# Halving the last query chunk and opening each new key chunk with half of its heads, in a two-layer attention kernel

## The chip, the cores and the metric

The kernel runs on one core of a Trainium2 chip. The metric is the time of one execution on the device, in microseconds. All comparisons are of runs in the fast state. A ratio is the mean time of one kernel's fast runs over that of the kernel before in the same rounds, so it is not quite the ratio of the medians quoted beside it.

## The reference

The computation is four residual blocks over x of 2048 tokens by 1024 features: a linear-attention block A, softmax attention B, A again with the same weights, B again. Each starts with a layer norm without parameters. Both have 32 heads of 32 dimensions.

```python
def _A_ref(x, wqkv, w_phi, wo):            # linear attention
    q, k, v = qkv[0], qkv[1], qkv[2]       # of x @ wqkv
    pq = jnp.einsum("bhsd,hdf->bhsf", q, w_phi)
    pk = jnp.einsum("bhsd,hdf->bhsf", k, w_phi)
    phi_q = concat([softmax(pq), softmax(-pq)])
    phi_k = concat([softmax(pk), softmax(-pk)])
    kv = jnp.einsum("bhsf,bhsd->bhfd", phi_k, v)
    ...                                    # num / (den + 1e-6)
    return o @ wo

def _B_ref(x, wqkv, wo):                   # softmax attention
    scores = jnp.einsum("bhqd,bhkd->bhqk", q, k) * (Dh ** -0.5)
    p = softmax(scores)
    o = jnp.einsum("bhqk,bhkd->bhqd", p, v)
    return o @ wo

x = x + _A_ref(_layernorm(x), ...); x = x + _B_ref(_layernorm(x), ...)   # twice
```

## The kernel before

Tokens are handled in four chunks of 512. A prologue computes A's keys for all four. Then each of two "layers" interleaves the query side of A, the projections of B, B's attention and the key side of the next A. VectorE, ScalarE, TensorE and GpSimd run in the order in which the program emits; the order of the DMA queue is left to a scheduler.

Attention is a generator. Every `yield` ends one *step*: eight score matmuls, two exponentials of 128x1024, and, two steps later, sixteen matmuls for numerator and denominator (`ND`). A group `g` is four heads; there are eight.

```python
def block(self, q, k0, k1, acc, oT, first, last, before=None):
    kv = self.load(k0, k1, 0, acc, first)          # K and V of group 0 from DRAM
    for g in range(G):
        if before and g in before:
            before[g]()                            # finish what group g needs
            kv = self.load(k0, k1, g, acc, first)
        nxt = None
        for half in range(2):                      # 256 queries
            for kc in range(0, k1 - k0, 2):
                self.step(...)
                if nxt is None and g + 1 < G and not (before and g + 1 in before):
                    nxt = self.load(k0, k1, g + 1, acc, first)
                yield
        kv = nxt
```

All the rest is also generators, which yield how many matmuls of 512 columns they emitted and whether a PSUM buffer ended. `Background` gives them a credit per step, and `until` forces one to its end while no attention runs.

```python
def pump(self, per):
    self.credit = min(self.credit + per, 8.0)
    ends = 0
    while self.credit > 0 and ends < PS["nb"]:
        got = self.next()
        ...
        self.credit -= got[0]
        ends += got[1]

def attend(att, block, bg, per):
    for _ in block:
        bg.pump(per)
        if len(att.lag) > 1:
            att.finish()
```

K and V go to DRAM (`kT_d`, `v_d`), 512 KB for 16 heads of a chunk, and attention loads them group by group. PSUM has three layouts, with S score tiles and NB buffers for everything else: wide (0, 8), mid (2, 3), narrow (3, 1). The schedule of a layer, cut to what matters:

```python
bg.add("b0", b_proj(0, (1,)))
bg.add("b1", rest1())                                            # chunk 1: K, V and queries, all heads
attend(att, att.block(qs[0], 0, 4, ..., {4: lambda: bg.until("b0")}), bg, 10)
settle(att)
bg.until("b1")
set_mode("narrow")
bg.add("b2", to_b(2))                                            # query side of A, norm, K and V of chunk 2
bg.add("b3", to_b(3))
attend(att, att.block(qs[0], 4, 8, acc[0], None, False, False), bg, 5)
attend(att, att.block(qs[1], 0, 8, acc[1], None, True, False), bg, 5)
bg.until("b2")
attend(att, att.block(qs[0], 8, 12, ...), bg, 6)
attend(att, att.block(qs[1], 8, 12, ...), bg, 6)
bg.until("b3")
for i in range(NCH):
    ...                                                          # add next query chunk and after(i - 1)
    block = (att.block(qs[i], 0, S // P, None, oT[i], True, True) if i > 1
             else att.block(qs[i], 12, 16, acc[i], oT[i], False, True))
    attend(att, block, bg, 3.5)
settle(att)
bg.until(f"after{NCH - 2}")
set_mode("wide")
drain(after(NCH - 1, oT[-1], layer, True))                       # exposed: nothing left to hide it under
```

`after` is the follow-up of a chunk: output projection, then in the first layer the norm and A's key side, in the second the transposed store. In the prologue the norm of the next chunk is merged into the key side of the current one: one end of the norm per four ends of the key side.

The softmax here doesn't subtract the row's maximum and nothing guards it: scores larger than these inputs give would overflow.

Of the kernel before, what the change touches and what calls it, by code (L numbers as in the profile page):

```python
# [19 lines left out]
P = 128  # L20
# [4 lines left out]
G = 8  # L25
# [7 lines left out]
def kernel(  # L33
# [140 lines left out]
    def mm8(ps, lhsT, rhs):  # L174
        for po in range(G):
            mm(ps, lhsT(po), rhs(po), po == 0, po == G - 1)
            if po == 3:
                yield 4, False
# [3 lines left out]
    def ln_gen(x, res, fast=False):  # L182
        ps = ps512()
        yield from mm8(ps, lambda po: ones_bf[:], lambda po: x[:, po, :])
        m = T("f", [P, C], F32)
        DVE.tensor_scalar(out=m[:], in0=ps, scalar1=1.0 / D, scalar2=None, op0=ALU.mult)
        yield 4, True
        xc = T("c8", [P, G, C], BF16)
        res["xc"] = xc
        sqs = []  # L190

        def centre(po):
            DVE.tensor_tensor(out=xc[:, po, :], in0=x[:, po, :], in1=m[:], op=ALU.subtract)  # L193

        ps = ps512()
        for po in range(G):
            centre(po)
            if po % 4 == 0:
                sq4 = T("st", [P, 4, C], BF16)
            sq = sq4[:, po % 4, :]  # L200
            if fast:
                SC.activation(out=sq, in_=xc[:, po, :], func=ACT.Square)
            else:
                DVE.tensor_tensor(  # L204
                    out=sq, in0=xc[:, po, :], in1=xc[:, po, :], op=ALU.mult
                )
            sqs.append(sq)
        yield from wait(3)
        for po in range(G):
            mm(ps, ones_bf[:], sqs[po], po == 0, po == G - 1)  # L210
            if po < G - 1 and po % 2:
                yield 2, False
        lnv = T("f", [P, C], F32)
        rstd = T("r", [P, C], F32)
        SC.activation(out=lnv[:], in_=ps, func=ACT.Ln, scale=1.0 / D, bias=eps_t[:])
        SC.activation(out=rstd[:], in_=lnv[:], func=ACT.Exp, scale=-0.5)
        yield 2, True

        diag = T("f", [P, 4, P], F32)
        rcol = T("rcol", [P, 4], F32)  # L220
        DVE.tensor_tensor(
            out=diag[:], in0=rstd[:].rearrange("p (t q) -> p t q", q=P),
            in1=ident[:].unsqueeze(1).to_broadcast([P, 4, P]), op=ALU.mult,
        )
        DVE.reduce_sum(out=rcol[:], in_=diag[:], axis=AX.X)
        if fast:
            ncol = T("nc", [P, 4], F32)
            DVE.tensor_scalar(
                out=ncol[:], in0=rcol[:], scalar1=-1.0, scalar2=None, op0=ALU.mult
            )  # L230
            res["ncol"] = ncol
        res["rstd"], res["rcol"] = rstd, rcol
        yield from wait(1)
# [15 lines left out]
    def ak_gen(c, x, get, fast=False, res=None, hook=None):  # L249
        if c == 0:  # L250
            kv_state["acc"] = [T(f"acc{i}", [P, 4, 258], F32) for i in range(2)]
# [5 lines left out]
        SP.dma_start(out=xa_d[c][:], in_=xc[:])  # L257
        SP.dma_start(out=ra_d[c][:], in_=rstd[:])
        va = []
        for i in range(2):  # L260
            v = T(f"acc{2 + 2 * (c % 2) + i}", [P, 2, G, P + 1], BF16)
            POOL.memset(v[:, :, :, P:P + 1], 1.0)
            va.append(v)
        for fc in range(2):
            w = get()
            for t in range(4):
                ps = ps512()
                yield from mm8(
                    ps, lambda po: xc[:, po, t * P:(t + 1) * P], lambda po: w[:, po, :]
                )  # L270
                scale_rows(
                    va[t // 2][:, t % 2, fc * 4:(fc + 1) * 4, 0:P],
                    ps.rearrange("p (g d) -> p g d", d=P), rcol[:, t:t + 1], fast,
                )
                yield 4, True
# [3 lines left out]
        for fc in range(2):  # L279
            w = get()  # L280
            es = []
            for t in range(4):
# [33 lines left out]
            def kv_part(fc=fc, es=es):  # L316
                for gi in range(4):
                    g = fc * 4 + gi
                    ps = ps512()
                    for t in range(4):  # L320
                        for s in range(2):
                            mm(
                                ps[:, s * 129:(s + 1) * 129],
                                es[t][:, s, gi * P:(gi + 1) * P],
                                va[t // 2][:, t % 2, g, :],
                                t == 0 and s == 0, t == 3,
                            )
                    if c == 0:
                        DVE.tensor_copy(out=kvacc[fc][:, gi, :], in_=ps[:, 0:258])
                    else:  # L330
                        DVE.tensor_tensor(
                            out=kvacc[fc][:, gi, :], in0=ps[:, 0:258], in1=kvacc[fc][:, gi, :],
                            op=ALU.add,
                        )
                    yield 2.5, True
# [114 lines left out]
    def aq_gen(c, x, slabs, res, pause=6):  # L450
        xr = aq_load(c)
        slabs.prefetch()
        es = [T("ea", [P, 2, C], BF16) for _ in range(G)]
        yield from aq_exp(xr, slabs.get, es)
        yield from aq_scale(es, res)
        yield from wait(pause)
        yield from aq_out(es, res)
        yield from aq_finish(c, x, slabs, res)

    def aq_finish(c, x, slabs, res):  # L460
        yield from proj_out(x, res["oT"], slabs)
        yield from ln_gen(x, res, PS["ns"] == 0)
        SP.dma_start(out=x_d[c][:], in_=x[:])

    def proj_out(x, oT, slabs):
        for ft in range(G):
            if ft % 4 == 0:
                w = slabs.get()
            ps = ps512()
# [4 lines left out]
            yield 4, True  # L474


    def bkv_gen(c, res, slabs, h, q=None):
# [24 lines left out]
        if q is not None:  # L502
            yield from bq_gen(q, xc, rstd, slabs, range(4 * h, 4 * h + 4))
# [13 lines left out]
    class Attention:  # L517
# [22 lines left out]
        def block(self, q, k0, k1, acc, oT, first, last, before=None):  # L540

            kv = self.load(k0, k1, 0, acc, first)
            for g in range(G):
# [4 lines left out]
                for half in range(2):  # L548
# [161 lines left out]
    def run():  # L710
# [19 lines left out]
        drain(ln_gen(xs[0], res, True))  # L730
        for c in range(NCH):
# [12 lines left out]
            main = ak_gen(c, xs[c], iter(av + pk).__next__, True, res, hook)  # L744
            if c + 1 < NCH:
                xs[c + 1] = load_first(c + 1)
                drain(merge(main, ln_gen(xs[c + 1], nres, True), 4))
# [5 lines left out]
        def after(c, oT, layer, fast=False):  # L753
            x = load_x(c)
            sl = Slabs(["bo"] + (["av", "pk"] if layer == 0 else []))
            sl.prefetch()
            yield from proj_out(x, oT, sl)
            if layer == 0:
                yield from ak_gen(c, x, sl.get, fast)
                SP.dma_start(out=x_d[c][:], in_=x[:])  # L760
            else:
                yield from store_out(c, x)
# [8 lines left out]
        for layer in range(2):  # L771
# [4 lines left out]
            BKVQ = ["bk0", "bv0", "bq0", "bk1", "bv1", "bq1"]  # L776

            def to_b(c):
# [4 lines left out]
                yield from b_proj(c, (0, 1))  # L783
                SP.dma_start(out=xb_d[c][:], in_=res["xc"][:])
                SP.dma_start(out=rb_d[c][:], in_=res["rstd"][:])

            def b_proj(c, parts):
                res = saved[c]
                for h in parts:
                    yield from bkv_gen(c, res, res["sl"], h, qs.get(c))  # L790
# [5 lines left out]
            r0["sl"] = Slabs(["ao"] + BKVQ)  # L796
            r1["sl"] = Slabs(["ao"] + BKVQ)
# [19 lines left out]
            drain(b_proj(0, (0,)))  # L817

            def rest1():
# [3 lines left out]
                yield from b_proj(1, (0, 1))  # L823

            bg = Background()
            set_mode("mid")
            bg.add("b0", b_proj(0, (1,)))
            bg.add("b1", rest1())
            acc = [([T(f"acc{k}", [P, 2, 2, QH], F32) for k in range(4)], 0), None]
            attend(  # L830
                att,
                att.block(qs[0], 0, 4, acc[0], None, True, False, {4: lambda: bg.until("b0")}),
                bg, 10,
            )
            settle(att)
            bg.until("b1")
            acc[1] = ([T(f"acc{4 + k}", [P, 2, 2, QH], F32) for k in range(4)], 1)
            set_mode("narrow")
            bg.add("b2", to_b(2))
            bg.add("b3", to_b(3))  # L840
            attend(att, att.block(qs[0], 4, 8, acc[0], None, False, False), bg, 5)
            attend(att, att.block(qs[1], 0, 8, acc[1], None, True, False), bg, 5)
            bg.until("b2")
            attend(att, att.block(qs[0], 8, 12, acc[0], None, False, False), bg, 6)
            attend(att, att.block(qs[1], 8, 12, acc[1], None, False, False), bg, 6)
            bg.until("b3")
            oT = [None] * NCH
            for i in range(NCH):
# [3 lines left out]
                if i:  # L852
# [3 lines left out]
                block = (  # L856
                    att.block(qs[i], 0, S // P, None, oT[i], True, True) if i > 1
                    else att.block(qs[i], 12, 16, acc[i], oT[i], False, True)
                )
                attend(att, block, bg, 3.5)  # L860
            settle(att)
            bg.until(f"after{NCH - 2}")
            set_mode("wide")
            drain(after(NCH - 1, oT[-1], layer, True))
# [99 lines left out]
    def store_out(c, x):  # L964
        for t in range(4):
# [6 lines left out]
            SP.dma_start(out=out[0, c * C + t * P:c * C + (t + 1) * P, :], in_=tr[:])  # L972
# [35 lines left out]
```

## Time and profile before

| | |
|---|---|
| median time | 2828.98 us (2825.19 to 2832.77, 2 runs) |
| profiled span | 2830.9 us |
| PE busy | 84% |
| ACT busy | 76% |
| DVE busy | 47% |

The prediction below reads the main lines. Three stretches that it doesn't show are needed later: query chunk 0 on key chunks 1, 2 and 3 in the first layer. The columns are the stretch, its length, busy time and count of PE, weight load, DVE, ACT and POOL, then the granted PE clock, the DMA share and GB/s.

```profile
412.00:489.40 77.40, 59.33 (x1112) 27.87 (x1114) 34.35 (x61) 67.59 (x80) 0.00 (x0) 0.89 0.31 95
624.00:702.00 78.00, 55.57 (x1006) 24.67 (x995) 37.71 (x67) 63.56 (x73) 0.00 (x0) 0.85 0.22 67
805.00:870.00 65.00, 46.59 (x772) 20.33 (x776) 45.03 (x62) 58.58 (x64) 0.17 (x1) 0.84 0.37 107
```

In each of them ACT is busy 81% to 90% of the time and PE 71% to 77%. The DMA engines are busy for 22% to 37% of it, so they are far from full.

In the prologue, the timeline of PE shows that the matmuls which sum the squares for the norms of chunks 2 and 3 run without a wait ahead of them:

```profile
102.86 1.89 PE L165 MATMUL BG<-st,ones 128*128 128x512 bf16 x8
137.59 1.89 PE L165 MATMUL BG<-st,ones 128*128 128x512 bf16 x8
```

### The profile page before, as it was taken

What the parts mean: (1) busy time and instruction counts of PE and PEld (TensorE: products, weight loads), DVE (VectorE), ACT (ScalarE), POOL (GpSimd) and SP (SyncE); (2) the same over time, 40 slices, a digit from 0 to 9 for tenths busy, and PEclk for the clock granted to TensorE, in tenths of its full rate; (3) what the DMA queues carried; (4) which work ended last, traced back from release to release, by engine and by line L of the source; (5) the groups of instructions that cost most, each with busy time, mean ns of one, the idle gap of its engine ahead of it and who ended that gap; (6) DMA issues with size and microseconds to landing.
All of it is one profiled execution on the core that took longest, in us unless ns stands there. A gap on an engine that the chain in (4) does not pass through costs nothing. (4 is left out here: it accounts for less than half of the span.)

```text
span 2830.9 us, 89391 instructions
## 1 busy us (share of the span) xinstructions
PE 2375.8 (84%) x40048; PEld 1151.2 (41%) x40048; DVE 1326.5 (47%) x2205; ACT 2156.5 (76%) x2489; POOL 95.7 (3%) x87
## 2 busy tenths in 40 slices
PE   7988997996778879888778899799777778988877
PEld 4543443442333444444334344344333334434333
DVE  5776544425457653454524745444443773323213
ACT  5543728997668889898894354699874889999996
POOL 1320000000000010010101000000000000000000
PEclk9999998998998999999999999999888899999999
DMA  8424363342443422323105154425234242221110
GB/s 241 127 88 137 122 192 98 136 136 64 151 130 89 150 96 84 125 77 125 62 17 175 45 187 140 140 70 188 85 103 159 83 125 91 92 76 47 52 41 16
DMA packets 231392, 308.48 MB, mean 109 GB/s; under 512 B 36640, under 2 KB 194336, under 8 KB 223840
## 3 DMA queue, kind: packets, MB, share of 16 engines
q1 hardware_dynamic: 230192, 301.20, 33.5%
q8 instruction: 313, 5.13, 0.7%
q10 hardware_dynamic: 816, 1.57, 0.2%
q14 instruction: 71, 0.58, 0.1%
HBM read 239.14 MB, written 58.33 MB: 105 GB/s over the span
## 5 line engine op out<-in xcount | busy, mean ns | idle before, releaser
L576 ACT ACTIVATE E<-S 128x1024 bf16<-128x1024 f32 x2048 | 1911.8, 1149 | 369.4 <-PE S L567 368.5
L594 PE MATMUL ND<-E,kv 128*32 128x256 bf16 x8192 | 652.5, 286 | 246.5 <-DVE dt L614 98.8
L567 PE MATMUL S<-q,kv 32*128 32x256 bf16 x8192 | 570.2, 283 | 79.5 <-ACT E L576 43.0
L594 PE MATMUL ND<-E,ones 128*32 128x256 bf16 x8192 | 589.6, 286 | 0.0
L169 PE MATMUL BG<-c,w 128*32 128x512 bf16 x7680 | 482.1, 385 | 33.4 <-DVE x L473 14.7
L594 PEld LDWEIGHTS <-kv 128*32 128x32 bf16 x8192 | 278.7, 99 | 496.0 <-issue 311.5
L567 PEld LDWEIGHTS <-kv 32*128 32x128 bf16 x8192 | 177.3, 93 | 406.1 <-issue 403.5
L594 PEld LDWEIGHTS <-ones 128*32 128x32 bf16 x8192 | 271.7, 100 | 54.1 <-issue 5.2
L169 PEld LDWEIGHTS <-w 128*32 128x32 bf16 x7680 | 191.4, 97 | 240.1 <-issue 107.2
L632 DVE RECIPROCAL rc<-nd 128x256 f32<-128x256 f32 x128 | 224.4, 1753 | 4.4
L169 PE MATMUL BG<-w,c 128*32 128x512 bf16 x3328 | 212.9, 388 | 12.1 <-DVE st L239 5.1
L473 DVE TENSOR_TENSOR x<-BG,x 128x512 bf16<-128x512 f32 x128 | 87.1, 689 | 193.7 <-PE BG L169 175.4
L625 DVE COPY nd<-ND 128x512 f32<-128x512 f32 x64 | 44.1, 689 | 260.9 <-PE ND L594 260.6
L165 PE MATMUL BG<-c,w 128*128 128x512 bf16 x640 | 150.6, 396 | 1.6 <-DVE nd L625 1.6
L169 PEld LDWEIGHTS <-c 128*32 128x32 bf16 x3328 | 83.8, 97 | 105.3 <-issue 46.8
L306 POOL TENSOR_TENSOR ea<-ea,sm 128x512 bf16<-128x512 bf16 x64 | 93.4, 1459 | 776.8 <-ACT E L576 328.1
L165 PEld LDWEIGHTS <-c 128*128 128x128 bf16 x704 | 69.3, 99 | 86.3 <-issue 6.6
L165 PE MATMUL BG<-w,c 128*128 128x512 bf16 x448 | 99.4, 383 | 2.0 <-ACT st L924 2.0
L300 DVE TENSOR_REDUCE sm<-ea 128x32 f32<-128x1024 bf16 x64 | 77.8, 1215 | 48.2 <-ACT ea L296 35.0
L165 PEld LDWEIGHTS <-w 128*128 128x128 bf16 x640 | 64.5, 101 | 85.3 <-issue 17.5
L387 DVE TENSOR_TENSOR f<-BG,r 128x512 f32<-128x512 f32 x64 | 43.3, 689 | 106.6 <-PE BG L169 76.7
L486 DVE TENSOR_TENSOR st<-BG,r 128x512 bf16<-128x512 f32 x64 | 44.2, 691 | 97.7 <-PE BG L169 93.3
(110 smaller groups left out, 1584.6 us busy)
## 6 DMA issues: line engine op xcount, KB each, us to landing
w<-in_B_wqkv_dram SPq DMA_DIRECT2D x48, 1024.0 KB
dn<-den_d SPq DMA_DIRECT2D x320, 64.0 KB
x_d<-x SPq DMA_DIRECT2D x16, 1024.0 KB
x<-x_d SPq DMA_DIRECT2D x16, 1024.0 KB
w<-in_A_wo_dram SPq DMA_DIRECT2D x16, 1024.0 KB
w<-in_B_wo_dram SPq DMA_DIRECT2D x16, 1024.0 KB
kv<-kT_d SPq DMA_DIRECT2D x32, 512.0 KB
kv<-v_d SPq DMA_DIRECT2D x32, 512.0 KB
```

The source lines that it names most:

```text
L165: PE.matmul(ps, lhsT=lhsT, rhs=rhs, start=start, stop=stop, skip_group_check=True)
L169: PE.matmul(ps[cols, :], lhsT=lhsT[:, cols], rhs=rhs, start=start, stop=stop, tile_position=(0, 32 * j), skip_group_check=True,)
L300: DVE.reduce_sum(out=ss[:], in_=e[:].rearrange("p s (h f) -> p s h f", f=DH), axis=AX.X)
L306: (POOL if s else DVE).tensor_tensor(out=e[:, s, :].rearrange("p (h f) -> p h f", f=DH), in0=e[:, s, :].rearrange("p (h f) -> p h f", f=DH ...
L387: DVE.tensor_tensor(out=pq[:], in0=ps, in1=rstd[:], op=ALU.mult)
L473: DVE.tensor_tensor(out=x[:, ft, :], in0=ps, in1=x[:, ft, :], op=ALU.add)
L486: DVE.tensor_tensor(out=st[:, gi, :], in0=ps, in1=rstd[:], op=ALU.mult)
L567: PE.matmul(tiles[j // 2][:, o:o + QH], lhsT=kv[rows, 0, (kc + k) * P:(kc + k + 1) * P], rhs=q[rows, g, half * QH:(half + 1) * QH], start= ...
L576: SC.activation(out=e[:], in_=tiles[i][:].rearrange("p (j k q) -> p j k q", k=2, q=QH), func=ACT.Exp, scale=SCALE,)
L594: PE.matmul(nd[rows, part * QH:(part + 1) * QH], lhsT=ones_bf[:, 0:32] if part else kv[:, 1, col:col + 32], rhs=es[j // 2][:, j % 2, i, :] ...
L625: DVE.tensor_copy(out=ndc[:], in_=nd[:])
L632: DVE.reciprocal(out=rc[:], in_=ndc[:, QH:C])
```

## The change

It has two parts and some retuned numbers. **Part 1**: the last query chunk is attended in two halves of 256 queries, so that the follow-up of its first half runs beside attention of the second; everything in that follow-up takes a width `n` and an offset `o`. **Part 2**: of each new key chunk only K and V of the first 16 heads are made before its attention starts; those of the other heads come in the background and are needed at group 4. The queries of query chunk 1 (64 units, in the prediction's sense of a unit: four tile matmuls over 512 columns) go to the background with them, as `q1`. The numbers: the norm yields five empty turns rather than three, `pause` goes from 6 to 8, the credit of two blocks from 6 to 5 and of the last chunk's blocks from 3.5 to 4.

```diff
     def ln_gen(x, res, fast=False):
+        n = x.shape[2]                      # widths C become n throughout
...
-        yield from wait(3)
+        yield from wait(5)
...
-    def aq_gen(c, x, slabs, res, pause=6):
+    def aq_gen(c, x, slabs, res, pause=8):
...
-        def block(self, q, k0, k1, acc, oT, first, last, before=None):
+        def block(self, q, k0, k1, acc, oT, first, last, before=None, halves=(0, 1)):
...
-            bg.add("b1", rest1())
+            bg.add("b1a", rest1())          # rest1 now ends with b_proj(1, 0)
...
-            bg.until("b1")
+            bg.until("b1a")
...
-            bg.add("b2", to_b(2))
-            bg.add("b3", to_b(3))
-            attend(att, att.block(qs[0], 4, 8, acc[0], None, False, False), bg, 5)
+            bg.add("b1b", b_proj(1, 1))
+            bg.add("q1", b_query(1))
+            bg.add("b2a", to_b(2))
+            bg.add("b2b", rest_b(2))
+            bg.add("b3a", to_b(3))
+            bg.add("b3b", rest_b(3))
+            attend(att, att.block(qs[0], 4, 8, acc[0], None, False, False, need("b1b")), bg, 5)
+            bg.until("q1")
             attend(att, att.block(qs[1], 0, 8, acc[1], None, True, False), bg, 5)
-            bg.until("b2")
-            attend(att, att.block(qs[0], 8, 12, acc[0], None, False, False), bg, 6)
-            attend(att, att.block(qs[1], 8, 12, acc[1], None, False, False), bg, 6)
-            bg.until("b3")
+            bg.until("b2a")
+            attend(att, att.block(qs[0], 8, 12, acc[0], None, False, False, need("b2b")), bg, 5)
+            attend(att, att.block(qs[1], 8, 12, acc[1], None, False, False), bg, 5)
+            bg.until("b3a")
...                                         # key chunk 3: need("b3b") for query chunk 0
+                    for half in range(2):   # i == 3
+                        if half:
+                            bg.add("after3", chain(wait(3), after(3, oT[3], layer, n=QH)))
+                        block = att.block(
+                            qs[i], 0, S // P, None, oT[i], True, True, halves=(half,)
+                        )
+                        attend(att, block, bg, 4)
             settle(att)
-            bg.until(f"after{NCH - 2}")
+            bg.until("after3")
             set_mode("wide")
-            drain(after(NCH - 1, oT[-1], layer, True))
+            drain(after(NCH - 1, oT[-1], layer, True, QH, QH))
```

## The prediction

> **What bounds the kernel now.** I read the page first (busy table, groups), then busy time by stretch, then the PE and DMA-queue timelines at the seams between stretches.
>
> ```profile
> PE 2375.8 (84%) x40048; PEld 1151.2 (41%) x40048; DVE 1326.5 (47%) x2205; ACT 2156.5 (76%) x2489; POOL 95.7 (3%) x87
> ...
> L576 ACT ACTIVATE E<-S 128x1024 bf16<-128x1024 f32 x2048 | 1911.8, 1149 | 369.4 <-PE S L567 368.5
> ```
>
> No engine is full over the whole span; the stretches differ. One attention "step" is two exponentials (L576), eight score matmuls (L567) and sixteen ND matmuls (L594); 512 steps make a layer. Between steps the kernel slips in background matmuls (BG).
>
> ```profile
> 489.40:624.00 134.60, 126.14 (x2611) 64.99 (x2612) 50.09 (x92) 124.33 (x139) 0.00 (x0) 1.00 0.43 140
> 702.00:787.00 85.00, 68.08 (x1397) 34.24 (x1398) 35.63 (x71) 61.81 (x66) 0.00 (x0) 0.92 0.46 145
> 787.00:805.00 18.00, 13.07 (x228) 6.28 (x224) 4.63 (x7) 0.00 (x0) 0.00 (x0) 1.00 0.47 147
> 1404.00:1495.50 91.50, 71.58 (x1192) 31.95 (x1185) 17.22 (x18) 91.49 (x100) 0.00 (x0) 1.00 0.08 25
> 1496.90:1563.30 66.40, 58.34 (x304) 27.96 (x304) 36.63 (x57) 21.79 (x34) 11.69 (x8) 0.89 0.54 186
> 2804.00:2831.00 27.00, 20.84 (x106) 9.64 (x97) 12.73 (x43) 0.00 (x0) 0.00 (x0) 0.82 0.10 39
> ```
>
> The columns are stretch, length, busy PE, weight load, DVE, ACT, POOL, then PE clock, DMA share and GB/s. 1404 to 1495 is attention alone: ACT is full, two exponentials take 1.83 us, and PE has room. 489 to 624 has both: PE 94%, ACT 92%. 787 to 805, 1497 to 1563 and 2804 to 2831 hold no attention at all; nor does 367 to 412, below. These are what the change attacks.
>
> ```profile
> 371.29 5.35 PE L169 MATMUL BG<-c,w 128*32 128x512 bf16 x96
> 376.47 7.07 PE L169 MATMUL BG<-w,c 128*32 128x512 bf16 x128
> 383.38 13.98 PE L169 MATMUL BG<-c,w 128*32 128x512 bf16 x256
> 397.19 7.07 PE L169 MATMUL BG<-w,c 128*32 128x512 bf16 x128
> 404.10 7.07 PE L169 MATMUL BG<-c,w 128*32 128x512 bf16 x128
> ...
> 791.75 1.91 PE L169 MATMUL BG<-c,w 128*32 128x512 bf16 x32 [0.79 <-DVE st L486]
> 794.45 1.91 PE L169 MATMUL BG<-w,c 128*32 128x512 bf16 x32 [0.79 <-DVE st L486]
> ```
>
> I call four tile matmuls over 512 columns a unit; a product of eight is eight units. Chunk 1's forced work, with three PSUM buffers, flows at 7.07 us for 32 units, **0.221 us a unit**. Chunk 3's, with one buffer, repeats every 2.70 us for eight units, **0.34 us a unit**, since PE waits 0.79 us for each copy-out. Within attention, consecutive starts of L567 in the PE timeline give 0.88 us for a step with no unit that nothing delays, 1.74 to 1.84 us with four and 2.71 us with eight: 0.88 + 0.22 a unit, but never under ACT's 1.83. So four units a step are free, and a unit above that costs as much as an exposed one.
>
> **What the Trainium skill says.** TensorE: Matmul & The Clock Gate, "Wait — 56ns, not 53.3ns?", has warm matmuls of 512 columns 215.7 ns apart; the trace's 0.221 agrees. PSUM — Partial Sum Buffer, "Engine vs sequencer instructions", has matmuls in program order and VectorE's queue as strict FIFO. The trace agrees: a scale chain queued on DVE stops PE for 8.2 us behind an unrelated accumulator.
>
> ```profile
> PE ND L594 <- DVE dt L614: 8.2, 1, 8.2
> ```
>
> DMA: Bandwidth & Descriptors, "Anatomy of one DMA — SWDGE (gpsimd) path", says that the fixed cost is mostly the receipt of the write, and worst into HBM. That path is not this queue's, but the trace shows a long round trip too: V's write to DRAM is issued at 276.21 and its read back at 283.69.
>
> ```profile
> 276.21 0.53 SPq L501 DMA_DIRECT2D v_d<-st  x1
> 283.69 1.51 SPq L526 DMA_DIRECT2D kv<-v_d  x2
> ```
>
> **The change part by part.** I counted units around each block of steps in the built order of PE, identical in both layers unless said. First those forced with no attention, in units: before chunk 1's keys (4 to 8) 192 becomes 64; before chunk 2's keys 4 becomes 52; before chunk 3's keys 60 becomes 124; between the layers 584 becomes 468; at the very end 72 becomes 36.
>
> *Part 1, the last query chunk in halves.* The follow-up of the first half runs under the second half's 64 steps, which had 44 units in layer 1 and 0 in layer 2, and get 160 and 36, always under four a step.
> - Between layers, 66.4 us are exposed (1496.9 to 1563.3: projection 15.3, norm 8.6, V 15.2, phi(K) and kv the rest). With 256 queries: projection 64 x 0.11 + 0.8 = 8, norm about 5, V 32 x 0.218 = 7, kv 2, four softmax tiles of 2.3 us on DVE with their start 12, end 3: 37 us. That saves 29. The six weight slabs are loaded twice, though, and some 9 MB must land in 37 us, 243 GB/s against the 186 here, so I take 26.
> - Hidden work isn't free. The whole follow-up of chunk 2 held 78 steps for 174.5 us, against 78 x 1.83 = 143: 31.5 over. Half, less something for the longer norm wait, is 13. Net for layer 1: -13.
> - Tail: 27.0 us. The projection halves from 16.5 to 8, transposes and stores go from 9.5 to 5.5: -13. Hiding 36 units costs about 1. Net: -12.
> - K/V loads for the chunk double (8 MB more a layer) where DMA is 8% busy: nothing.
>
> Sum of part 1: **-25 us**.
>
> *Part 2, K/V of 16 heads first, for each layer.*
> - Before chunk 1's keys: 45.0 us from score to score become 0.88 + 64 x 0.221 = 15: -30.
> - Before chunk 2's: 52 x 0.34 = +17.
> - Before chunk 3's: 20.4 becomes 40 x 0.34 for the projection, 68 x 0.34 for K/V, and between them a norm whose 16 DVE operations and two PE passes nobody covers, about 14: 51. +30.
> - In the five blocks the counts are 86, 261, 58, 153, 0 before and 156, 168, 132, 56, 60 after, for 32, 64, 32, 32, 32 steps. Stepping through the new order with the durations of like steps of before (1.83; 2.10 mean at five units; 2.44 with a query-feature exponential; 10 for each scale chain), the blocks go from 77, 134, 77, 83, 65 to 75, 133, 83, 64, 70 us: -12. The 128 moved units push chunks 2 and 3 back by 26 steps, and what no longer fits reappears, slower, in the two later gaps.
>
> Sum: -30 + 17 + 30 - 12 = +5 a layer, **+10**. The longer waits (five for three in the norm, eight for six) spare perhaps 4 a layer of stalls such as the 2.9 us for squares in chunk 1: **-8**.
>
> **The rivals.**
> - *A DRAM round trip takes the place of the wait removed.* Before, the query projection (32 units, 7 us) or other heads' K/V stood between V's write and its first use. Now V is the last thing made before the first step of chunks 1, 2 and 3, and again at group 4 of chunk 3. 7.5 us from write to read and up to 3 for the read, less 3.5 of steps that PE can do, is 7 us each time, 28 a layer, 56 in all. For it: strict order on PE, and the build waits on that landing. Against: part of the 7.5 us was a 1 MB weight load issued just before. I take a third, **+18**. In full, the kernel lands near 2862.
> - *ACT is the bound throughout, and hidden work is free.* Then part 1 gains its 26 + 13 = 39 without the 14 of cost, and the blocks of part 2 shed some 15 more a layer, which turns +5 into -10: about -59, near 2770. Against: steps with five units already take 2.10 us, above 1.83.
> - *Weight traffic at the layer's end becomes the bound*, and the halved follow-up saves 15 rather than 26: +10 on my figure. DMA share was 0.54 there.
>
> **Range and chances.** -25 + 10 - 8 + 18 = -5: 2829 - 5 = **2824 us**. The round trip alone spans 0 to 56, the ACT rival reaches 2770; 2775 to 2870 should hold eight times in ten. 2% is 57 us, so faster needs nearly everything well: 0.14. Slower by 57 needs the full round trip and a failed part 1: 0.10. Within 2%: 0.76.
>
> **What would show it.** Right: no attention for about 15 us before chunk 1's keys, 17 before chunk 2's, 50 before chunk 3's; 40 rather than 66 us between last exponential and next layer's features; a tail near 14. Right for the rival: PE idle before the first ND of those blocks, ended by the V load. Wrong: gap three under 35 us, or second-half steps of the last chunk well above 1.95 us. A slot order on the DMA queue that holds K/V back would make me wrong towards slow; denominators landing earlier, hence fewer DVE stalls, towards fast.

## The result

The changed kernel takes 2912.19 us (2910.93 to 2913.46, 2 runs) against 2828.98 us: ratio 1.0294, interval 1.0232 to 1.0356. It is slower by 2.9%, outside the range that the prediction gave. The span of the profiled run is 2909.0 us against 2830.9, 78 us more. The interval is wide, some 18 us to either side, because each kernel ran only twice here. I found where the time went by the first and last exponential of each block of attention in the two traces (query chunk 0 on key chunk 0 in the first layer takes 87 us in both and is left out):

| stretch | before, us | after, us | difference |
|---|---|---|---|
| start to first attention step | 282.6 | 300.5 | +17.9 |
| layer 1: forced before key chunk 1 | 42.9 | 17.1 | -25.8 |
| layer 1: query chunk 0 on key chunk 1 | 76.9 | 90.7 | +13.8 |
| layer 1: query chunk 1 on key chunks 0 and 1 | 134.4 | 138.7 | +4.3 |
| layer 1: forced before key chunk 2 | 0.8 | 16.4 | +15.6 |
| layer 1: query chunk 0 on key chunk 2 | 77.2 | 90.8 | +13.6 |
| layer 1: query chunk 1 on key chunk 2 | 84.8 | 64.3 | -20.5 |
| layer 1: forced before key chunk 3 | 18.5 | 50.2 | +31.7 |
| layer 1: query chunk 0 on key chunk 3 | 65.4 | 84.1 | +18.7 |
| layer 1: rest of attention | 625.3 | 634.4 | +9.1 |
| between the layers | 162.7 | 135.4 | -27.3 |
| layer 2: first attention step to the end of query chunk 0 | 595.7 | 629.9 | +34.2 |
| layer 2: rest of attention | 549.8 | 550.4 | +0.6 |
| after the last step | 27.5 | 18.7 | -8.8 |

So part 1 gave what was promised (-27.3, -8.8, +9.1, +0.6). The prologue lost 18 us, and the stretch of part 2, from the first attention step to the end of query chunk 0, lost 52 us in the first layer (587.9 to 640.0) and 34 in the second.

The stretches of the changed kernel that answer to those of before, in the same columns: query chunk 0 on key chunk 1, the gap before key chunk 2, query chunk 0 on key chunk 2, the gap before key chunk 3, query chunk 0 on key chunk 3, the seam between the layers and the tail.

```profile
404.00:496.00 92.00, 74.58 (x1424) 35.46 (x1428) 24.85 (x50) 64.48 (x72) 0.00 (x0) 0.89 0.41 125
633.00:650.60 17.60, 12.60 (x224) 6.28 (x216) 4.39 (x6) 1.88 (x2) 0.00 (x0) 1.00 0.32 101
650.60:742.00 91.40, 67.78 (x1310) 33.00 (x1307) 32.68 (x59) 67.99 (x81) 0.00 (x0) 0.87 0.40 121
804.00:856.00 52.00, 34.62 (x520) 15.04 (x520) 20.39 (x35) 3.49 (x5) 0.00 (x0) 0.90 0.44 148
856.00:940.50 84.50, 56.31 (x1032) 25.86 (x1032) 49.66 (x69) 59.83 (x65) 0.00 (x0) 0.82 0.40 120
1574.60:1612.00 37.40, 30.38 (x192) 17.81 (x192) 20.81 (x40) 11.47 (x23) 5.06 (x4) 0.88 0.74 248
2890.40:2909.00 18.60, 12.45 (x94) 9.31 (x93) 8.37 (x27) 0.00 (x0) 0.00 (x0) 0.76 0.07 28
```

In the fifth line, key chunk 3, no engine is near full: PE 67%, ACT 71%, DVE 59%, for 84.5 us in place of 65. Something is waited for. The waits of PE in that stretch are, first before, then in the changed kernel (in all, times, longest, in us):

```profile
PE ND L594 <- DVE nd L630: 12.9, 14, 5.1
```

```profile
PE ND L595 <- DMA kv<-v_d: 15.2, 2, 9.8
PE ND L595 <- DVE nd L631: 6.0, 8, 2.1
```

A wait for the load of V has appeared, 15.2 us in two places. From the first attention step to the end of query chunk 0, PE's waits for V are four in each layer, 23.7 and 22.7 us; with those for K just written it is 29.0 and 28.1 us, 57 in all, where the kernel before has none. In the timeline of PE they are the first numerator of the block and that of group 4; the third line is from later in the timeline:

```profile
858.15 1.05 PE L169 MATMUL BG<-c,w 128*32 128x512 bf16 x16
864.57 0.40 PE L595 MATMUL ND<-E,kv 128*32 128x256 bf16 x4 [5.38 <-DMA kv<-v_d]
...
911.89 0.41 PE L595 MATMUL ND<-E,kv 128*32 128x256 bf16 x4 [9.84 <-DMA kv<-v_d]
```

The timeline of the DMA queue shows V written and read back around them, and one earlier case (447.15) for comparison. The columns are the start, the issue time, and what is issued.

```profile
439.00 0.53 SPq L116 DMA_DIRECT2D w<-wpq_d  x1
...
447.15 0.39 SPq L504 DMA_DIRECT2D v_d<-st  x1
...
450.32 0.33 SPq L527 DMA_DIRECT2D kv<-v_d  x1
...
854.18 0.37 SPq L116 DMA_DIRECT2D w<-in_B_wqkv_dram  x1
854.97 0.36 SPq L504 DMA_DIRECT2D v_d<-st  x1
...
862.42 0.33 SPq L527 DMA_DIRECT2D kv<-v_d  x1
```

The read wants what was just written, so it waits for the write to land; from the issue of the one to the issue of the other it is 7.45 us at 854.97, but only 3.17 us at 447.15. The difference to the eye is the 1 MB weight load, issued 0.8 us ahead in the slow case and 8 us ahead in the quick one. I come back to this.

The gap before key chunk 3 is 50 us, because 124 units are now forced there. PE is neither starved of data nor at its rate:

```profile
816.01 1.91 PE L169 MATMUL BG<-c,w 128*32 128x512 bf16 x32 [0.79 <-DVE x L476]
...
822.60 0.40 PE L169 MATMUL BG<-st,ones 128*32 128x512 bf16 x4 [1.98 <-DVE st L201]
...
841.24 1.91 PE L169 MATMUL BG<-c,w 128*32 128x512 bf16 x32 [0.79 <-DVE st L489]
```

Products wait 0.79 us each for the copy-out of the single buffer, and the norm in the middle waits for squares made on VectorE.

In the prologue the same matmuls over squares as before now wait:

```profile
109.36 3.57 PE L165 MATMUL BG<-st,ones 128*128 128x512 bf16 x8 [8.08 <-DVE acc L333]
155.44 3.57 PE L165 MATMUL BG<-st,ones 128*128 128x512 bf16 x8 [8.08 <-DVE acc L333]
```

Twice 8.08 us of idle PE, and the matmuls after it take 3.57 in place of 1.89 us. That makes up the 18 us.

Those slower matmuls point to something that the prediction and the experiments leave out. In the columns of before, here are two stretches in which the granted clock of the changed kernel, the third number from the end, was halved:

```profile
104.48:114.72 10.24, 5.36 (x13) 1.86 (x13) 4.93 (x10) 1.32 (x2) 3.10 (x4) 0.50 0.00 1
862.24:869.07 6.83, 4.50 (x64) 1.81 (x64) 0.87 (x2) 1.94 (x2) 0.00 (x0) 0.50 0.56 169
```

Both begin inside a wait of PE (8.08 us, ended at 109.36, and 5.38 us, ended at 864.57) and last beyond it, so such a wait costs more than its own length here. Over the stretch of part 2 the same number of matmuls keeps PE busy for 505 us a layer, against 491 and 496 before: 23 of the 86 us lost in the two layers, and 61 are longer idle time of PE.

### The profile page after: what moved, and what is told of

Its sections match the earlier page's. It is cut to its first block, busy times and chain, and to the rows that moved or that the text cites. A ratio compares the mean times of both kernels' runs of the same rounds, so it can differ in the third digit from the quotient of the medians.

```text
span 2909.0 us, 91345 instructions
## 1 busy us (share of the span) xinstructions
PE 2374.3 (82%) x40960; PEld 1164.8 (40%) x40960; DVE 1342.6 (46%) x2256; ACT 2153.7 (74%) x2487; POOL 95.7 (3%) x87
## 5 line engine op out<-in xcount | busy, mean ns | idle before, releaser
L595 PE MATMUL ND<-E,kv 128*32 128x256 bf16 x8192 | 641.4, 285 | 255.5 <-DVE dt L615 60.7
L568 PE MATMUL S<-q,kv 32*128 32x256 bf16 x8192 | 555.1, 283 | 83.7 <-ACT E L577 41.5
L169 PE MATMUL BG<-c,w 128*32 128x512 bf16 (+1 forms) x8192 | 523.6, 388 | 50.1 <-DVE x L476 23.7
L169 PEld LDWEIGHTS <-w 128*32 128x32 bf16 x8192 | 208.5, 98 | 273.4 <-issue 154.9
L169 PE MATMUL BG<-w,c 128*32 128x512 bf16 x3584 | 231.4, 389 | 34.5 <-DVE st L237 19.2
L476 DVE TENSOR_TENSOR x<-BG,x 128x512 bf16<-128x512 f32 (+1 forms) x144 | 89.6, 630 | 211.5 <-PE BG L169 199.5
L169 PEld LDWEIGHTS <-c 128*32 128x32 bf16 x3584 | 90.6, 97 | 133.3 <-issue 73.6
L165 PE MATMUL BG<-c,w 128*128 128x512 bf16 (+1 forms) x640 | 139.8, 381 | 3.5 <-DVE c L634 1.9
L165 PEld LDWEIGHTS <-w 128*128 128x128 bf16 x640 | 66.7, 105 | 74.5 <-issue 15.6
L514 DVE TENSOR_TENSOR q<-BG,r 128x512 bf16<-128x512 f32 x64 | 44.1, 690 | 107.9 <-PE BG L169 85.7
L437 DVE TENSOR_TENSOR ea<-BG,ea 128x512 bf16<-128x512 f32 x96 | 64.1, 687 | 51.8 <-PE BG L169 51.8
```

The source lines that it names most:

```text
L165: PE.matmul(ps, lhsT=lhsT, rhs=rhs, start=start, stop=stop, skip_group_check=True)
L169: PE.matmul(ps[cols, :], lhsT=lhsT[:, cols], rhs=rhs, start=start, stop=stop, tile_position=(0, 32 * j), skip_group_check=True,)
L437: DVE.tensor_tensor(out=es[g][:, s, :], in0=ps, in1=es[g][:, s, :], op=ALU.mult)
L476: DVE.tensor_tensor(out=x[:, ft, :], in0=ps, in1=x[:, ft, :], op=ALU.add)
L514: DVE.tensor_tensor(out=q[:, g, :], in0=ps, in1=rstd[:], op=ALU.mult)
L568: PE.matmul(tiles[j // 2][:, o:o + QH], lhsT=kv[rows, 0, (kc + k) * P:(kc + k + 1) * P], rhs=q[rows, g, half * QH:(half + 1) * QH], start= ...
```

## The experiments

Twelve kernels were run, three rounds each. Where a rival is put to the test, the comparison is by ratio to the kernel before, since runs were made in several lots. All were correct except the four that are wrong on purpose. One gap: `pause` and the credit of the blocks on key chunk 2 were never put back by themselves. They count as part of part 2 below; key chunk 1 alone, which has the old ones, loses 60 us all the same.

### Part 1 alone

The kernel before with the halves; norm wait 3, and K/V, pauses and credits of part 2 as before.

```diff
-            drain(after(NCH - 1, oT[-1], layer, True))
+            ...                             # all of part 1, nothing of part 2
+            drain(after(NCH - 1, oT[-1], layer, True, QH, QH))
```

> The kernel before with the last query chunk in halves alone (norm wait three, old order of K/V, old pauses). Theory (parts add up; traces give 9 more in the block, 27 less between the layers, 9 less at the tail): 26 to 28 us faster than before, 2802, ratio 0.991. Rival (halving costs more once the rest is as before, since the follow-up of chunk 2 then has no slack): ratio 0.996 or more.

Measured: 2810.33 us against 2833.53, ratio 0.9913 (0.9897 to 0.9930), that is 25 us. The theory holds.

### Part 2 alone

The changed kernel without the halves, norm wait 3.

```diff
-                        attend(att, block, bg, 4)      # in two halves
+                attend(att, block, bg, 3.5)            # whole, as before
...
-        yield from wait(5)
+        yield from wait(3)
```

> The changed kernel without the halves and with norm wait three: K/V of the first 16 heads first, alone. Theory (the whole loss beyond the prologue is here): 52 and 34 us from the two layers, 2829 + 86 = 2915, ratio 1.030. Rival (half of that loss comes from the longer norm wait or from the double weight loads): under 2880, ratio under 1.018.

Measured: 2915.69 us, ratio 1.0289 (1.0274 to 1.0305), 82 us lost. The theory holds: what remains of the loss apart from the prologue is in part 2, and neither the norm's turns nor the doubled weight loads of part 1 are needed for it.

### The norm's two turns

```diff
-        yield from wait(5)
+        yield from wait(3)
```

> The changed kernel with one number put back: the norm yields three empty turns, not five. Theory (the two added turns push the next chunk's norm past the end of the merged prologue, where PE then idles 8.1 us twice): the first attention step starts at 282 us again instead of 300, the kernel loses about 18 us against the changed one, 2894, ratio to before 1.023. Rival (the later start has another cause, or the wait saves as much inside attention as it costs in the prologue, as the prediction had it): 2905 to 2915, ratio 1.027 or more.

Measured: 2883.82 us, ratio 1.0176 (1.0159 to 1.0194). The two turns cost 1.18% of 2829, 33 us, more than the theory's 18; this is uncertain by some 18 us, because of the changed kernel's two runs, and the two profiled spans differ by 32. The prologue did regain its 18 (first step at 282.7 us). The trace has another 15 us less in layer 1 up to the end of query chunk 0 and 3 in layer 2, spread over several blocks and gaps, while the rest of layer 1 is 4 us longer; I did not separate these further. The prologue's matmuls run without the wait again:

```profile
101.31 1.89 PE L165 MATMUL BG<-st,ones 128*128 128x512 bf16 x8
136.04 1.89 PE L165 MATMUL BG<-st,ones 128*128 128x512 bf16 x8
```

The reason can be counted in the program. For chunks 1 and 2 the key side has 24 ends, so the merged norm gets six turns. With three empty turns it has six: mean, three empty, squares, column sums. With five it has eight, and its last two, squares and column sums, come after the key side has ended, with nothing beside them.

### K and V from an old place

Wrong on purpose: query chunk 0 on key chunks 1, 2 and 3 loads K and V of the same size from the places of key chunk 0.

```diff
         def block(self, q, k0, k1, acc, oT, first, last, before=None, halves=(0, 1)):
+            if before:
+                k0, k1 = 0, k1 - k0
```

> The changed kernel, wrong on purpose: query chunk 0 on key chunks 1, 2 and 3 loads the same amount of K and V from the places of key chunk 0, which were written long before; forced work, order and bytes are the same. Theory (the DRAM round trip of K/V made just before use costs some 29 us a layer in waits of PE for kv, and some of the late denominators behind it): 60 us less than the changed kernel, near 2852, ratio 1.008. Rival (the loss is work pushed into the gaps, where one PSUM buffer makes it slow): less than 20 us gained, ratio 1.022 or more.

Measured: 2870.73 us, ratio 1.0131 (1.0116 to 1.0147). Against the changed kernel's 1.0294 that is 1.63%, **46 us** gained: between the two, much nearer the theory. It is again uncertain by some 18 us; the two profiled spans differ by 38, and the stretch of part 2 by 26 us in the first layer and 20 in the second. In the stretch in which V was waited for before, PE's waits are now:

```profile
PE ND L597 <- DVE nd L633: 12.7, 10, 4.8
```

The wait for kv is gone, and a part of it has come back as one for DVE, for denominators, about as long as in the kernel before (12.9). So more than half of part 2's loss is the round trip, but the rival has a share as well: in layer 1, from the first attention step to the end of query chunk 0, this kernel takes 613.9 us, the changed one 640.0 and the one before 587.9. Of the 26 us that are left, the gaps make 21 (-27.6, +15.6, +33.3) and the blocks of attention 3. In layer 2, where 14 us are left, the gaps make 20 and the blocks are 7 shorter than before.

### The same in the kernel before

A control, wrong on purpose in the same way.

```diff
-            attend(att, att.block(qs[0], 4, 8, acc[0], None, False, False), bg, 5)
+            attend(att, att.block(qs[0], 4, 8, acc[0], None, False, False, None, True), bg, 5)
...                                         # True: read the places of key chunk 0; three blocks
```

> Control for the wrong-on-purpose run: the kernel before, whose query chunk 0 on key chunks 1, 2 and 3 loads K and V from the places of key chunk 0. Theory (before, other work stood between writing K/V and using it, so there was no round trip to save): within 8 us of before, ratio 0.997 to 1.000. Rival (reading the old places is cheaper by itself, and the 42 us gained in the changed kernel are no measure of a wait): 20 us or more gained, ratio 0.993 or less.

Measured: 2827.03 us, ratio 0.9986 (0.9966 to 1.0006). Reading the old places is worth nothing where no round trip is waited for.

### Small weight slabs

Why is the round trip so long? The DMA queue's timeline pointed at weights issued just ahead. This kernel is the changed one with norm wait 3, wrong on purpose: beside attention every slab loads 128 KB, not 1 MB.

```diff
+                if PS["mode"] != "wide":
+                    SP.dma_start(out=w[:, 0:1, :], in_=W[n](h)[:, 0:1, :])
+                    w = FirstRows(w)        # every product reads slice 0
+                else:
                     SP.dma_start(out=w[:], in_=W[n](h))
```

> The changed kernel with norm wait three, wrong on purpose: beside attention each weight slab loads one eighth (128 KB) of its 1 MB, and all eight products of a group use that eighth; same matmuls, same forced work, V's round trip still there. Theory (7 to 8.5 us from V's write to its read because a 1 MB weight load is issued about 1 us before the write; 3 us where it is issued 6 us or more before): the trips fall to 3 to 4 us, four a layer, 28 to 34 us gained against the 2884 of the same kernel with full slabs: 2852, ratio 1.006. Rival (the trip is a fixed cost of writing to DRAM and reading back): 10 us or less gained beyond the control, ratio 1.014 or more.

Measured: 2808.67 us, ratio 0.9922 (0.9907 to 0.9937), 72 us less than with full slabs (1.0176). That is twice what the theory asked. The round trip at the start of key chunk 3 in this run's DMA queue, with its weight load still 0.8 us ahead:

```profile
801.75 0.33 SPq L124 DMA_DIRECT2D w<-in_B_wqkv_dram  x1
802.54 0.37 SPq L515 DMA_DIRECT2D v_d<-st  x1
807.30 0.32 SPq L538 DMA_DIRECT2D kv<-v_d  x1
```

4.76 us, where the same kernel with full slabs took 8.03 and the changed kernel 7.45. The others of the same layer are 3.0, 4.5, 3.2 and 3.4 us, and one of 5.1 that was 3.0 with full slabs. In layer 1 up to the end of query chunk 0 the idle time ahead of PE's matmuls, added up by what ended it, falls from 24.4 to 11.1 us for kv, and from 48.1 to 41.7 for denominators of DVE. The stretch as a whole shrinks by 27 us, and 16 of these are in query chunk 0 on key chunk 1.

Not all of the 72 us is waiting, though. Over the stretch of part 2 in both layers this kernel takes 63 us less than with full slabs, and 22 of them are the same matmuls done in less time, at a higher granted clock: 0.94 against 0.92 and 0.91, and in query chunk 0 on key chunk 1 1.00 against 0.89. In the control below, against the halves alone, that part is 5 us. Whether the clock is higher because PE waits less, or for another reason of these runs, was not tested.

### Small weight slabs where nothing waits

The control: the same edit on part 1 alone.

> Control for the small slabs, wrong on purpose in the same way: the halves alone, where nothing waits for K/V just written. Theory: the weights were hidden, 0 to 8 us gained against the halves alone, ratio 0.9885 to 0.9915. Rival (less DMA traffic speeds everything, denominators above all): 20 us or more gained, ratio 0.984 or less.

Measured: 2792.00 us, ratio 0.9862 (0.9846 to 0.9879). Against the halves alone (0.9913) that is 0.51%, 14 us: more than the theory's 8, less than the rival's 20. So lighter weights gain something even without part 2. Net of this control, the small slabs give 1.0176 - 0.9922 - 0.0051 = 2.03%, **57 us**, of the 1.0176 - 0.9913 = 2.63%, 74 us, that part 2 costs with norm wait 3. The 17 us that are left, 0.60%, are lost even with light weights. By the traces some 17 of the 57 are the matmuls at a higher clock; the slabs also lighten all weight traffic, and not only the loads ahead of V, so the 57 is not the cost of those loads by themselves.

### Key chunk 1 alone

Part 1, and of part 2 only key chunk 1.

```diff
-                yield from b_proj(1, (0, 1))
+                yield from b_proj(1, (0,))
...
+            bg.add("b1b", b_proj(1, (1,)))
+            bg.add("q1", b_query(1))
             bg.add("b2", to_b(2))
```

> The halves alone, and of the other part only key chunk 1: K/V of its first 16 heads forced, the rest and the second query chunk beside attention; chunks 2 and 3 whole, as before. Counted in the built order: the forced work before key chunk 1 falls from 192 to 64 units, that before chunk 2 rises from 4 to 100 and before chunk 3 from 60 to 104. Theory (work is only pushed on, from gaps at 0.22 us a unit to gaps at 0.34, and the round trip comes on top): -27 + 33 + 15 for the gaps, +11 for waits in chunk 1's block, -14 for lighter blocks: 18 a layer lost against the halves alone, 2846, ratio 1.004. Rival (chunk 1 is where the idea pays and chunk 2 is what spoils it): faster than the halves alone, ratio under 0.989.

Measured: 2868.47 us, ratio 1.0124 (1.0096 to 1.0153), 60 us worse than the halves alone: 30 a layer where 18 were expected. The direction of the theory holds, and the rival is out. The gaps before key chunks 2 and 3 of the first layer, in the columns of before:

```profile
616.10:648.30 32.20, 22.66 (x388) 10.84 (x383) 8.56 (x12) 0.02 (x1) 0.00 (x0) 1.00 0.51 152
807.00:840.10 33.10, 23.82 (x416) 11.66 (x412) 8.96 (x13) 0.01 (x2) 0.00 (x0) 1.00 0.50 152
```

32 and 33 us, against 0.8 and 18.5 in the halves alone, pay back more than the 26 saved before key chunk 1 (42.4 to 16.8). That accounts for +20 in layer 1; the blocks of query chunk 0 and 1 on key chunk 1 add 18, where the theory had 11 for waits, and the lighter blocks after them give back 4, where it had 14.

### Three buffers in the gaps

The changed kernel with norm wait 3; the forced work before key chunks 2 and 3 runs in the layout with three buffers.

```diff
+    def forced(att, bg, name):              # ends the product under way first
+        settle(att)
+        set_mode("mid")
+        bg.until(name)
+        set_mode("narrow")
...
-            bg.until("b2a")
+            forced(att, bg, "b2a")
-            bg.until("b3a")
+            forced(att, bg, "b3a")
```

> The changed kernel with norm wait three, and what is forced before key chunks 2 and 3 done with three PSUM buffers in place of one (attention drained, other layout, back). Theory (a good part of what remains is work displaced into gaps that run at 0.34 us a unit for want of a buffer): some 168 units a layer at 0.22 save 20, less 3 for draining twice: 30 us for two layers, 2854 against the 2884 of the same kernel without it, ratio 1.007. Rival (the gaps are bound by the norm's chain and by weights arriving, not by the buffer): under 10 us, ratio 1.014 or more.

Measured: 2857.34 us, ratio 1.0098 (1.0074 to 1.0123), 22 us gained by ratio where 30 were expected and the rival had under 10. The gap before key chunk 3 goes from 48.1 to 38.2 us and the one before key chunk 2 from 13.6 to 11.8. In the timeline of PE the last of the forced products now follow each other without a wait:

```profile
807.50 7.09 PE L169 MATMUL BG<-w,c 128*32 128x512 bf16 x128
```

7.09 us for 32 units, 0.22 a unit. The norm in the gap is as slow as before; it sits on VectorE.

### The halves, with three buffers before key chunk 3

The same function in part 1 alone, for the 60 units forced there.

```diff
-            bg.until("b3")
+            forced(att, bg, "b3")
```

> The halves alone, with K/V as in the kernel before, and the 60 units forced before key chunk 3 done with three PSUM buffers. Theory (copy-out of the single buffer, 0.79 us in each 2.7, is what they wait for): 18.5 us of gap become 14 with draining, 5 a layer, 10 in all: 2800, ratio 0.988. Rival (draining attention costs what the buffers give): 2810, ratio 0.991.

Measured: 2789.45 us, ratio 0.9852 (0.9833 to 0.9871), 17 us better than the halves alone. The gap fell about as expected, 18.5 to 15.0. The rest I had not foreseen: query chunk 0 on key chunk 3 fell from 64.9 to 60.5 us in the first layer and from 65.7 to 61.6 in the second, its ACT at 96% to 98%. Whether that is because the drained attention leaves its denominators landed earlier wasn't tested.

### Key chunk 3 alone

Part 1, and of part 2 only key chunk 3, at five units a step.

```diff
-            bg.add("b3", to_b(3))
+            bg.add("b3", to_b(3, (0,)))
+            bg.add("b3b", rest_b(3))
...
-                    attend(att, block, bg, 3.5)
+                    attend(att, block, bg, 3.5 if i else 5)
```

> The halves alone, and of the other part only key chunk 3: its attention opens with the first 16 heads, and the other heads' K/V run beside it at five units a step. The forced 60 units become 4. Theory (round trip): the gap of 18.5 falls to about 3, but PE waits for V of the first heads some 7 us and again some 8 at group 4, and VectorE is near full in that block (+6): between -3 and +5 a layer, ratio 0.989 to 0.995. Rival (without displaced work the idea pays as intended): 12 or more a layer gained, ratio 0.983 or less.

Measured: 2778.00 us, ratio **0.9813** (0.9797 to 0.9829), 28 us better than the halves alone and the best of all. My theory falls here, and the rival holds: 14 us a layer. The 60 forced units became 4, with nothing behind them to be displaced. And the round trip was short; here the weight load came after the write:

```profile
783.14 0.39 SPq L504 DMA_DIRECT2D v_d<-st  x1
783.62 0.45 SPq L116 DMA_DIRECT2D w<-in_B_wqkv_dram  x1
786.65 0.34 SPq L529 DMA_DIRECT2D kv<-v_d  x1
```

3.51 us, and PE waited 2.6 us for V in that block, once. The same kernel's write of the other heads' V, with a weight load issued 0.8 us ahead, took 8.3 us to its read. But at group 4 PE did not wait at all: at five units a step the other heads' V was written long enough before.

### Key chunk 3, and the second query chunk as a cover

```diff
-            r1["sl"] = Slabs(["ao"] + BKVQ)
+            r1["sl"] = Slabs(["ao"] + ["bk0", "bv0", "bq", "bk1", "bv1"])
...
+            bg.add("b1b", b_proj(1, (1,)))
             bg.add("b2", to_b(2))
```

> A try for a better version: key chunk 3 opened with its first heads as in the run that gained, and for key chunk 1 the second query chunk's projection forced right after the first heads' V (it covers the round trip), so that only 64 units move into attention. Counted: 128, 32 and 36 units forced before chunks 1, 2 and 3, against 192, 4 and 4. Theory (displaced units cost 0.34 us instead of 0.22): -14 + 9 + 11 and about -4 in the blocks, 0 to 5 a layer lost against the run with chunk 3 alone, ratio 0.982 to 0.985. Rival (what hurts is the round trip alone, and the cover removes it): 10 a layer gained, ratio 0.975.

Measured: 2796.01 us, ratio 0.9871 (0.9849 to 0.9892), 16 us worse than with key chunk 3 alone. The rival is out: even with its round trip covered, moving work out of the gap before key chunk 1 costs more than it brings. The loss of 8 a layer is above the 0 to 5 of the theory. About 3 of the 8 are a longer wait for V at key chunk 3 (5.9 us against 2.6 in layer 1, 4.5 against 1.1 in layer 2), where the weight load was again issued ahead of the write, by 0.8 us; at key chunk 1 PE did not wait for V.

## Why the prediction was wrong

The sum on record was -25 + 10 - 8 + 18 = -5. Its terms, one by one:

- **Part 1, -25: right.** Alone it measured 25 us. The seam between the layers was put at 37 us and 243 GB/s; the trace shows 38.2 us (PE from 1576.05 to 1614.23) and 248 GB/s. The tail went only to 18.7 where 14 were written, and this was made up by the seam and by the blocks of the last chunk, so that the sum came out so close is in part luck.
- **Longer waits, -8: wrong in sign.** The norm's two turns cost 33, give or take 18; the longer `pause`, which the term also holds, was not measured by itself. The prediction looked at the stall that three turns leave inside attention and did not carry the two new turns through the merged prologue, where the number of turns is limited. That was to be had from the program alone, and the 18 us of the prologue are shown by the trace and by putting the number back. The other 15 are measured but not explained.
- **The round trip, +18 ("I take a third"): right in kind, wrong in weight.** The rival's full figure was 56, eight trips of 7; in the trace PE waits for V in eight places, 46 us in all, and 11 us for K, 57 together, and taking them away gives 46. The reason I discounted it, that part of the 7.5 us was a weight load issued just ahead, is true, and it does not help, because in the changed kernel a weight load is issued just ahead of nearly every such write: the same projection that ends with V has just freed a slab. In the DMA queue after, ten such round trips took 6.4 to 8.6 us with a load 0.5 to 1.7 us ahead, and two 3.2 us with the load 7 to 8 us ahead; with norm wait 3, two with the load 2.4 us ahead took 4.3 and 4.5. The Trainium skill's page DMA: Bandwidth & Descriptors, section "Anatomy of one DMA — SWDGE (gpsimd) path", gives a fit of 2.0 us plus bytes over 436 GB/s: for 512 KB an estimate from it is 3.2 us, which is what the undisturbed write took here up to the issue of its read, though on another path; with 1 MB more in front the estimate is 5.6, and the trace has 6.4 to 8.6.
- **Work moved, +10: too small.** The gaps are as worked out: -26, +16, +32 in the trace against -30, +17, +30. The blocks of attention are not. Apart from the round trips they were to be 12 us shorter a layer (11 by the prediction's own list, 436 to 425), and with the old places they are 3 longer in layer 1 and 7 shorter in layer 2. The step that failed is to price the steps of a block by like steps of before. Why they are longer stays open: later denominators are not it, since PE's waits for these add up to 56 and 53 us with the old places, against 62 and 66 before. Net of the round trips the term is some 28 to 36 (74 - 46 with the halves, 82 - 46 without), not 10; how much of it is displaced work and how much late transfers is not settled, since with small slabs only 17 of the loss of part 2 are left.

The -25 of the sum stood, and the rest came to +33 for the waits, +46 for the round trip and +28 for what else part 2 does: together 82, against the 83 measured. That it closes proves little, since the 28 was got by subtraction.

Of the rivals, the DRAM round trip was the one to believe, and the sign that the prediction named for it, PE idle before the first ND ended by the V load, is the line at 864.57. ACT as the bound was wrong, and weight traffic at the seam was not an obstacle. Weight traffic in front of V was, by the small slabs and by the order of loads and writes in the DMA queue; no run moved those loads alone.

PSUM — Partial Sum Buffer, "Engine vs sequencer instructions", in the Trainium skill says that matmuls start in program order. This is why a wait for one group's V stops everything: before 864.57 PE did none of the scores and background products that come later in its order, for 5.38 us. The trace agrees with the page.

## What to carry to other kernels

Before moving work out of an exposed gap, ask where it lands: here a unit cost 0.22 us in the gap that it left and 0.34 us in the later gap into which it pushed others, and only the move at the end of the queue, with nothing behind it, paid. When data goes through DRAM to its consumer, keep at least a round trip's worth of other work between them, and keep bulk loads from being issued just ahead of the write. An empty turn added to a generator is free only where the loop that drives it has turns to spare, so count them in every place in which it is used.

## What the Trainium skill lacked or had wrong

- DMA: Bandwidth & Descriptors, "Anatomy of one DMA — SWDGE (gpsimd) path": its fit is of a transfer by itself. What a small write pays behind a bulk load isn't in it: 512 KB took 3.0 to 3.7 us from issue of the write to issue of the read with no 1 MB load just ahead, and 6.4 to 8.6 us with one, where an estimate by the fit for both together is 5.6.
- TensorE: Matmul & The Clock Gate, "Wait — 56ns, not 53.3ns?": its 215.7 ns holds for four tile matmuls side by side (0.221 us), but only with buffers to spare. With one PSUM buffer the same product took 0.34 us a unit, and with three 0.22. No page that I read gives a figure for that.
